# Attention rows in token order, and the first GLU tile's LayerNorm inside the last forward segment

## Chip, cores and metric

One core of a Trainium2 chip runs the whole program: forward and backward of one transformer block in one launch. The metric is the device time in us of that launch. The kernel before takes 3122.28 us (median of 3 runs, 3121.11 to 3123.98).

## The reference

The block has a recurrent attention with memory, and a gated GLU; both branches are modulated by a condition vector. The kernel gives the output and the gradients of all inputs. Cut to what matters here:

```python
# attention: 64 segments of 32 tokens; 8 memory rows go from each segment to the next
for s in range(n_seg):
    h = concat([mem, x[:, s*32:(s+1)*32]])            # 40 rows
    q, k, v = h@Wq, h@Wk, h@Wv                        # 32 heads of 128
    o = softmax(mask(q k^T * scale)) v @ Wo
    mem = o[:, :8]
    outs.append(o[:, 8:])                             # 32 rows of the branch's output
# block
h = layernorm(x) * (1 + ca) + sa
x = x + ga * attention(h)
h = layernorm(x) * (1 + cb) + sb
x = x + gb * ((sigmoid(h @ w_gate) * (h @ w_up)) @ w_down)
# and jax.vjp of all of it with grad_out
```

x is 1 x 2048 x 512, the GLU's inner width F is 1792, and all tensors are bfloat16.

## The kernel before, in words

The program has four stages: the forward loop over the segments (`phase2`), the GLU forward and backward (`phase3`), the backward loop over the segments (`phase4`) and the weight gradients of the attention (`phase5`).

**Forward loop.** 64 segments follow one another, since each needs the memory rows of the one before. A segment projects K, Q and V (L771 to L785), turns K and Q, multiplies and exponentiates (`st_exp`), sums and divides (`den`, `pv`, `ost`), turns the result (`ott`) and multiplies by Wo (`outproj`, L849). TensorE works on 32 rows a segment: the 8 memory rows and the first 24 tokens. The last 8 tokens of four segments are collected and multiplied together (`TailRows`). The result of a segment is split into a high and a low bfloat16 part (`split_pair`, at_hi and at_lo), folded (`sum_pair`), and in the next segment turned into rows and stored by `store_rows` (L336) through POOL's queue: 32 rows of a segment into `AOA`, and 32 tail rows of four segments into `AOB`. So the rows of one GLU tile of 128 tokens lie in eight pieces. The instructions of the forward loop keep the order of the program on each engine (`pin`, L894).

**Between the loops.** In segment 63 SP queues the four rows of the modulation, broadcast to 128 partitions in float32 (`mod_bc` of 2 to 5: ga, sb, cb, gb), and the loads of GLU tile 0 (L793 to L796). POOL queues the loads of w_down, w_up and w_gate into the memory of Wv and Wk, which the projections no longer need (L810 to L812). The last probabilities and values are turned on TensorE (L882 to L891), and the last tail rows are finished (L892).

**GLU.** 16 tiles of 128 tokens go through a software pipeline of seven steps s0 to s6; a round runs the deepest step first (`run_pipeline`). s0 loads the next tile (`glu_load`: dout, eight pieces of attention rows, x0), makes the residual x1 and its LayerNorm on DVE, and db = grad_out * gb on POOL. s1 turns h2 and db by DMA into hdT. s2 makes g and u (32 products of 448 columns for each tile, by L1039 and L1043), s3 the backward product du (L1062, evacuated by DVE in L1064), s4 the forward product by w_down and pr_gb = dout * b on DVE (L1089), s5 the product by the turned w_up and w_gate, and the LayerNorm's backward, s6 column sums in `acc_ps`. The backward products need w_down, w_up and w_gate turned: 168 turns of 128 x 128 on TensorE (`wdT_piece`, `wT_piece`), placed in s0 of tiles 0 to 2 (L974). In phase 3 only DVE, ACT and POOL are held behind the forward loop (`pin_behind`, L1182); the order of the rest comes from the scheduler of the build.

**After the GLU.** `accs` (L1183) takes the column sums out of PSUM and goes to DMOD. The memory of phase 3 is then used again, for the turned Wo (WoT) among others.

Of the kernel before, what the change touches and what calls it, by code (L numbers as in the profile page):

```python
# [10 lines left out]
ALU = mybir.AluOpType  # L11
# [29 lines left out]
class K:  # L41
# [43 lines left out]
    def alloc_dram(self):  # L85
# [6 lines left out]
        self.AOA = d("AOA", [NS + 1, 32, cfg.D], BF16)  # L92
        self.AOB = d("AOB", [NS // 4, 32, cfg.D], BF16)
# [231 lines left out]
    def store_rows(self, psp, pool, ft, dram, name, tag, then=None):  # L325
# [5 lines left out]
        def f():  # L331
            tp = psp.tile([128, 128], BF16, name=name + "_tp", tag=tag)
            nc.tensor.transpose(tp[:], tb[:], self.ident[:])
            rb = pool.tile([128, 128], BF16, name=name + "_rb")
            nc.vector.tensor_copy(rb[:], tp[:])
            nc.gpsimd.dma_start(dram.rearrange("r (c x) -> (r c) x", x=128), rb[:])  # L336
            if then is not None:
                then(rb)
# [93 lines left out]
    def phase2(self):  # L432
# [13 lines left out]
        with ExitStack() as ctx:  # L446
# [26 lines left out]
            nc.gpsimd.dma_start(self.AOA[0, 0:M, :], io["A_mem0"].rearrange("o m d -> (o m) d"))  # L473
# [174 lines left out]
            tail = TailRows(self, sb2, psp, psp, 1, "ao", self.AOB, 2, ptag="p")  # L648
# [20 lines left out]

            i0 = len(self.traced())  # L670
            for pi in range(NP):
                mask_mm(pi)
            for s in range(NS):
# [95 lines left out]
                if norms:  # L769
                    norms.pop()()  # L770
                proj("k", 0, "dve")  # L771
                proj("k", 1, "act")
                if s == 0:
                    for f in firsts["k"]:
                        f()
# [17 lines left out]
                if s == NS - 1:  # L793
                    for i in range(2, 6):
                        self.mod_bc(None, i, "", t=self.bcs[i])
                    self.glu_first = self.glu_load(0, nc.sync)  # L796
# [12 lines left out]
                else:  # L809
                    nc.gpsimd.dma_start(self.w_down, io["B_w_down"].rearrange("(fc p) d -> p fc d", p=128))  # L810
                    nc.gpsimd.dma_start(self.w_up, io["B_w_up"].rearrange("(c p) f -> p c f", p=128))
                    nc.gpsimd.dma_start(self.w_gate, io["B_w_gate"].rearrange("(c p) f -> p c f", p=128))  # L812
# [44 lines left out]
                parts = self.split_pair(sb2, at_ps, "at")  # L857
                tail.collect(s4, [OT])
# [11 lines left out]
                self.store_rows(psp, sb2, ft, self.AOA[s + 1], "at", "p")  # L870
# [9 lines left out]
                if s < NS - 1:  # L880
                    norms.append(norm)
            for pi in range(NP):  # L882
# [9 lines left out]
            tail.finish()  # L892
            nc.vector.tensor_scalar_add(self.bcs[4], self.bcs[4], 1.0)
# [18 lines left out]
    def glu_load(self, j, q):  # L912
        io, D = self.io, self.cfg.D
        r0, r1 = j * 128, (j + 1) * 128
        x0, a_rows, dout = self.ring_x0[j % 2], self.ring_a[j % 6], self.ring_dout[j % 7]
        q.dma_start(dout, io["grad_out"].rearrange("o s d -> (o s) d")[r0:r1, :])
        self.load_x_rows(a_rows, j, self.AOA[1:], self.AOB, q)
        q.dma_start(x0, io["A_x"].rearrange("o s d -> (o s) d")[r0:r1, :])
        return dict(x0=x0, a_rows=a_rows, dout=dout)

    def phase3(self):
# [9 lines left out]
        with ExitStack() as ctx:  # L931
# [32 lines left out]
            def wdT_piece(c):  # L964
                def f():
                    for f0 in range(0, FC, 7):
# [7 lines left out]
            pieces = {0: [wdT_piece(c) for c in range(DC)],  # L974
                      1: [wT_piece(w_up, w_upT, 0, 8, 0), wT_piece(w_up, w_upT, 8, 6, 0)],
                      2: [wT_piece(w_gate, w_gateT, 0, 8, 1), wT_piece(w_gate, w_gateT, 8, 6, 1)]}
# [3 lines left out]
            def load(j):  # L980
                if j >= NT or j in ins:
                    return
                ins[j] = self.glu_first if j == 0 else self.glu_load(j, nc.sync)

            def s0(j):
                r0, r1 = j * 128, (j + 1) * 128
                load(j + 1)
                for f in pieces.pop(j, []):
                    f()
                st = ins.pop(j)  # L990
                a_rows = st["a_rows"]
                t0 = sbp.tile([128, D], F32, name="t0", tag="f32tmp", bufs=5)
                nc.vector.tensor_tensor(t0[:], a_rows[:], ga_bc[:], op=ALU.mult)
                x1 = sbp.tile([128, D], F32, name="x1", bufs=4)
                nc.vector.tensor_tensor(x1[:], t0[:], st["x0"][:], op=ALU.add)
                sts = sbp.tile([128, 6], F32, name="st", bufs=2)
                nc.vector.bn_stats(sts[:], x1[:])
                mv = sbp.tile([128, 2], F32, name="mv", bufs=2)
                nc.vector.bn_aggr(mv[:], sts[:])
                ve = sbp.tile([128, 1], F32, name="ve3", bufs=2)  # L1000
                nc.vector.tensor_scalar_add(ve[:], mv[:, 1:2], EPS)
                rstd = sbp.tile([128, 1], F32, name="rstd2", bufs=6)
                i0 = len(self.traced())
                nc.gpsimd.tensor_tensor(rstd[:], ve[:], mhalf[:], op=ALU.pow)
                db = sbp.tile([128, D], BF16, name="db", bufs=2)
                nc.gpsimd.tensor_tensor(db[:], st["dout"][:], gb_bc[:], op=ALU.mult)
                self.pin(i0, [mybir.EngineType.Pool])
                nc.gpsimd.dma_start(self.DBROWS[r0:r1, :], db[:])
                xh2 = sbp.tile([128, D], BF16, name="xh2", bufs=5)
                xhf = sbp.tile([128, D], F32, name="xhf", tag="f32tmp", bufs=5)  # L1010
                nc.vector.tensor_scalar(xhf[:], x1[:], mv[:, 0:1], rstd[:, 0:1], op0=ALU.subtract, op1=ALU.mult)
                nc.scalar.activation(xh2[:], xhf[:], AF.Copy)
                h2a = sbp.tile([128, D], F32, name="h2a", tag="f32tmp", bufs=5)
# [1079 lines left out]
```

The softmax here doesn't subtract the row's maximum and nothing guards it: scores larger than these inputs give would overflow.

## Time and profile before

| | |
|---|---|
| time, median of 3 | 3122.28 us |
| span of the profiled execution | 3125.4 us |
| PE busy | 3004.2 us, 96% |
| DVE, ACT, POOL busy | 52%, 40%, 47% |
| DMA busy in the forward loop (60 to 980 us) | 0.80 to 0.81 of 16 engines |
| forward loop ends | about 995 us |
| last product of the GLU's pipeline | about 1380 us |

A line of a timeline gives the start and the duration in us, the engine, the line of the kernel, the operation, output and inputs, shapes and count, and in brackets how long the engine stood idle before it and what ended that. SPq is SP's queue of DMA issues. A line of the table by stage gives the stretch, its length, then busy us and number of instructions for PE, its weight loads (PEld), DVE, ACT and POOL, the granted clock of TensorE, the busy share of the DMA engines and GB/s. In names of tiles, Wv, Wk and Wq stand for everything that lies in their memory in the GLU: w_down, the modulation rows and the rings of x0 and attention rows in Wv, w_gate and w_up in Wk, the turned w_gate and w_up in Wq.

### The profile page before, as it was taken

How to read it: one execution, taken by the hardware profiler on the slowest of the kernel's cores; microseconds unless marked ns; L12 is line 12 of the kernel's file. 1: busy time of each engine (PE TensorE's matmuls, PEld its weight loads, DVE VectorE, ACT ScalarE, POOL GpSimd, SP SyncE). 2: the span in 40 equal slices, each digit the busy share in tenths (PEclk: the TensorE clock that was granted, in tenths of full speed). 3: DMA queues.
4: the chain of work that ended last, by engine and by line, in shares of the span. 5: the costliest groups of instructions: out<-in, count | busy, mean ns of one | idle time of the engine just before them, and what ended most of it. 6: DMA issues, size and time to landing. Idle time of an engine off the chain costs nothing.

```text
span 3125.4 us, 106126 instructions
## 1 busy us (share of the span) xinstructions
PE 3004.2 (96%) x43769; PEld 1838.1 (59%) x43845; DVE 1616.2 (52%) x3738; ACT 1264.6 (40%) x3053; POOL 1473.0 (47%) x2974
## 2 busy tenths in 40 slices
PE   5999999999998799989989999999999999999999
PEld 3666666666665444445567777777777754455454
DVE  4556656655654777733255555555655542322321
ACT  2555555555554433322155555555555530110111
POOL 3666666666665466531144444444444432233322
PEclk8999999999999899999999999999999999999999
DMA  8887788788787798898589999999999998666674
GB/s 295 214 214 199 205 214 212 204 207 213 205 207 237 177 214 219 202 267 271 185 218 244 240 248 242 244 243 248 244 239 244 243 270 285 201 202 213 196 234 147
DMA packets 844665, 703.54 MB, mean 225 GB/s; under 512 B 543794, under 2 KB 716370, under 8 KB 843796
## 3 DMA queue, kind: packets, MB, share of 16 engines
q1 hardware_dynamic: 714404, 486.69, 62.2%
q0 software_dynamic: 59120, 148.64, 14.6%
q10 hardware_dynamic: 70656, 61.41, 6.3%
q8 instruction: 345, 5.65, 0.8%
q14 instruction: 140, 1.15, 0.1%
HBM read 294.93 MB, written 276.35 MB: 183 GB/s over the span
## 4 chain that ended last, share of the span: by engine, by line
PE 50%; issue 4%; DMA 2%; POOL 1%; DVE 0%; SPq 0%; ACT 0%; POOLq 0%; DVEq 0%
PE gps L1885 10%; PE dh_ps L216 8%; PE g_ps L1547 6%; PE pass_ps L256 5%; PE gps5o L1899 4%; PE dhq_ps L224 4%; PE gps L1234 3%; PE dh_tps L216 3%; PE dp_ps L1526 2%; PE tps L1459 2%; PE dp_ps L1534 1%; PE turn_ps L1413 1%; PE dh_ft L321 1%; PE gps L1164 1%; PE wtp L1300 1%
## 5 line engine op out<-in xcount | busy, mean ns | idle before, releaser
L1885 PE MATMUL gps<-rows,hrows 128*128 128x512 bf16 (+2 forms) x2124 | 415.6, 355 | 1.9
L1885 PEld LDWEIGHTS <-hrows 128*128 128x128 bf16 x2160 | 211.2, 98 | 204.6
L256 PEld LDWEIGHTS <-hT 128*32 128x32 bf16 x6144 | 158.2, 97 | 161.3 <-issue 1.9
L1591 POOL COPY dOst<-RAd 96x512 bf16<-96x512 bf16 x128 | 75.4, 613 | 311.3 <-DVE RAd L63 311.1
L1889 POOL DMA_DIRECT2D out_dram<-ot x108 | 81.4, 754 | 258.6 <-DVE ot L63 132.3
L63 DVE CAST ot<-gps 128x512 bf16<-128x512 f32 (+3 forms) x76 | 48.1, 633 | 284.9 <-PE gps L1885 191.6
L875 POOL TENSOR_TENSOR Pst<-Pst,rden 120x1408 bf16<-120x1408 bf16 x63 | 159.6, 2533 | 57.4 <-issue 38.9
L61 ACT ACTIVATE ot<-gps 128x512 bf16<-128x512 f32 (+3 forms) x75 | 41.3, 551 | 356.2 <-PE gps L1885 225.3
L61 ACT ACTIVATE dVT<-g_ps 128x512 bf16<-128x512 f32 (+1 forms) x192 | 109.3, 569 | 95.9 <-PE g_ps L1547 95.5
L63 DVE CAST RA0v<-pass_ps 128x512 bf16<-128x512 f32 x128 | 88.5, 692 | 89.5 <-PE pass_ps L256 86.2
L216 PE MATMUL dh_ps<-WvT,dVT 128*32 128x512 bf16 x2048 | 133.4, 380 | 0.0
L256 PE MATMUL pass_ps<-Wv,hT 128*32 128x512 bf16 x2048 | 133.3, 380 | 0.0
L1899 PE MATMUL gps5o<-WoT,rows 128*128 128x512 bf16 x580 | 127.8, 379 | 1.0 <-DMA rows<-OSR 0.3
L224 PE MATMUL at_ps<-Wo,OT 128*32 128x256 bf16 x4096 | 125.0, 275 | 0.1
L256 PE MATMUL pass_ps<-Wk,hT 128*32 128x512 bf16 x2048 | 123.3, 383 | 1.5 <-ACT hT L865 1.1
L1536 DVE SCALAR_TENSOR_TENSOR dS<-dp_ps,Pst_l 128x512 bf16<-128x512 f32 (+1 forms) x192 | 112.0, 639 | 22.8 <-PE dp_ps L1534 22.8
L256 PE MATMUL pass_ps<-WoT,dyT 128*32 128x256 bf16 (+1 forms) x3072 | 122.4, 308 | 0.9 <-ACT dyT L1665 0.9
L224 PE MATMUL dhq_ps<-WqT,dQT 128*32 128x256 bf16 x4096 | 122.9, 273 | 0.0
L216 PE MATMUL dh_ps<-WkT,dKT 128*32 128x512 bf16 x2048 | 122.3, 380 | 0.0
L256 PE MATMUL pass_ps<-Wq,hT 128*32 128x512 bf16 x2048 | 121.6, 379 | 0.0
L224 PEld LDWEIGHTS <-dQT 128*32 128x32 bf16 x4096 | 109.6, 97 | 15.9
L709 ACT ACTIVATE ET<-st_ps 128x480 bf16<-128x480 f32 (+1 forms) x192 | 96.1, 535 | 42.6 <-ACT qT L61 34.7
(419 smaller groups left out, 7164.5 us busy)
## 6 DMA issues: line engine op xcount, KB each, us to landing
OSR<-Ost SPq DMA_DIRECT2D x64, 352.0 KB
OT<-OT SPq DMA_DIRECT2D x64, 352.0 KB
VT<-VTr SPq DMA_DIRECT2D x64, 352.0 KB
PS<-Pst SPq DMA_DIRECT2D x64, 352.0 KB
OT_l<-OT SPq DMA_DIRECT2D x64, 352.0 KB
Pst_l<-PS SPq DMA_DIRECT2D x64, 352.0 KB
VT_l<-VT SPq DMA_DIRECT2D x64, 352.0 KB
DVR<-rows_x POOLq DMA_DIRECT2D x64, 352.0 KB, 6.4
```

The source lines that it names most:

```text
L61: return nc.scalar.activation(out, in_, AF.Copy)
L63: return nc.vector.tensor_copy(out, in_)
L216: self.nc.tensor.matmul(ps[32 * j:32 * j + 32, :], lhsT=lhsT, rhs=w, start=(n < 4), stop=(n >= total - 4), tile_position=(0, 32 * j))
L224: nc.tensor.matmul(ps[32 * j:32 * j + 32, :], lhsT=x[k], rhs=w[k][:, 256 * d:256 * d + 256], start=(n == 0), stop=(n == total - 1), tile_p ...
L256: self.nc.tensor.matmul(ps[32 * j:32 * j + 32, :], lhsT=lhs(c), rhs=rhs, start=(c == 0), stop=(c == DC - 1), tile_position=(0, 32 * j))
L709: nc.scalar.activation(part3(ET, pi)[:, 0:n, 0:120], st_ps[:, 0:n, 0:120], AF.Exp, scale=cfg.scale)
L875: nc.gpsimd.tensor_tensor(Pst[0:120, :, :], Pst[0:120, :, :], rden[:, :].unsqueeze(2).to_broadcast([120, G, 128]), op=ALU.mult)
L1234: nc.tensor.matmul(ps[:], lhsT=h2r[:, j, c * 128:(c + 1) * 128], rhs=xr[:, j, :], start=(j == 0), stop=(j == NT - 1))
L1536: nc.vector.scalar_tensor_tensor(out=part3(dS, pi), in0=ps[:, 0:n, :], scalar=cfg.scale, in1=part3(Pst, pi), op0=ALU.mult, op1=ALU.mult)
L1547: nc.tensor.matmul(ps[:, j, :], lhsT=lh[:, g * GW:(g + 1) * GW], rhs=rh[:, g * GW:(g + 1) * GW], start=True, stop=True)
L1885: nc.tensor.matmul(ps[:, 0:ng * E], lhsT=hrows[:, tp_, c * 128:(c + 1) * 128], rhs=rows[:, tp_, 0:ng * E], start=(tp_ == 0), stop=(tp_ == ...
L1899: nc.tensor.matmul(pss[gg][:], lhsT=src[0][:, src[1], gg * E:(gg + 1) * E], rhs=dyrows[:, tp_, :], start=(tp_ == order[0]), stop=(tp_ == o ...
```

## The change

1. **Rows in token order.** `AOA` and `AOB` become `AOM` (the memory rows of each segment) and `AX` (all tokens in order). The stores go through SP: two for a segment, four for the tail of four segments. A GLU tile's attention rows are then one load instead of eight. The loads of `glu_load` are in the order x0, attention rows, dout.
2. **First tile inside segment 63.** LayerNorm and turns of GLU tile 0 (`glu_first`) are written into segment 63, behind the split of its attention result. They use memory of Wq, which is free after the Q projection. It is meant to have hdT of tile 0 ready before PE asks for it.
3. **Weights and turns reordered.** w_gate and w_up are loaded right after segment 63's K projection, w_down after its first P·V product. The turns come as w_gate, w_down, w_up, one part after each round of the pipeline, instead of w_down, w_up, w_gate in the first three rounds.
4. **Smaller moves.** `tail.finish` stands before the last turns; pr_gb moves from s4 to s5 (2 buffers instead of 3); `accs` lies in Wk's memory.

```diff
-        self.AOA = d("AOA", [NS + 1, 32, cfg.D], BF16)
-        self.AOB = d("AOB", [NS // 4, 32, cfg.D], BF16)
+        self.AOM = d("AOM", [NS + 1, cfg.M, cfg.D], BF16)
+        self.AX = d("AX", [cfg.S, cfg.D], BF16)
...
+            def rows_a(rb, s):
+                c_x = lambda t: t.rearrange("r (c x) -> (r c) x", x=128)
+                nc.sync.dma_start(c_x(self.AOM[s + 1]), rb[0:M * DC, :])
+                nc.sync.dma_start(c_x(self.AX[s * T:s * T + 32 - M, :]), rb[M * DC:128, :])
+            def rows_b(rb, b):
+                for i in range(4):
+                    t = (4 * b + i + 1) * T
+                    nc.sync.dma_start(self.AX[t - M:t, :].rearrange("r (c x) -> (r c) x", x=128), rb[32 * i:32 * i + 32, :])
...
-                if norms:
+                if s < NS - 1 and norms:
                     norms.pop()()
                 proj("k", 0, "dve")
                 proj("k", 1, "act")
+                if s == NS - 1:
+                    nc.gpsimd.dma_start(self.w_gate, io["B_w_gate"].rearrange("(c p) f -> p c f", p=128))
+                    nc.gpsimd.dma_start(self.w_up, io["B_w_up"].rearrange("(c p) f -> p c f", p=128))
+                    norms.pop()()
...
                 if s == NS - 1:
-                    for i in range(2, 6):
+                    self.glu_st = self.glu_load(0, nc.sync)
+                    for i in (2, 4, 3, 5):
                         self.mod_bc(None, i, "", t=self.bcs[i])
-                    self.glu_first = self.glu_load(0, nc.sync)
...
                     nc.gpsimd.dma_start(self.w_down, io["B_w_down"].rearrange("(fc p) d -> p fc d", p=128))
-                    nc.gpsimd.dma_start(self.w_up, io["B_w_up"].rearrange("(c p) f -> p c f", p=128))
-                    nc.gpsimd.dma_start(self.w_gate, io["B_w_gate"].rearrange("(c p) f -> p c f", p=128))
...
                 parts = self.split_pair(sb2, at_ps, "at")
+                if s == NS - 1:
+                    nc.vector.tensor_scalar_add(self.bcs[4], self.bcs[4], 1.0)
+                    self.glu_first(small)
                 tail.collect(s4, [OT])
...
-                self.store_rows(psp, sb2, ft, self.AOA[s + 1], "at", "p")
+                self.store_rows(psp, sb2, ft, lambda rb, s=s: rows_a(rb, s), "at", "p")
...
+            tail.finish()
             for pi in range(NP):
                 ps, n = transposes_part(ET, pi)
...
-            tail.finish()
-            nc.vector.tensor_scalar_add(self.bcs[4], self.bcs[4], 1.0)
...
+        q.dma_start(x0, io["A_x"].rearrange("o s d -> (o s) d")[r0:r1, :])
+        q.dma_start(a_rows, self.AX[r0:r1, :])
         q.dma_start(dout, io["grad_out"].rearrange("o s d -> (o s) d")[r0:r1, :])
-        self.load_x_rows(a_rows, j, self.AOA[1:], self.AOB, q)
-        q.dma_start(x0, io["A_x"].rearrange("o s d -> (o s) d")[r0:r1, :])
...
-            pieces = {0: [wdT_piece(c) for c in range(DC)],
-                      1: [wT_piece(w_up, w_upT, 0, 8, 0), wT_piece(w_up, w_upT, 8, 6, 0)],
-                      2: [wT_piece(w_gate, w_gateT, 0, 8, 1), wT_piece(w_gate, w_gateT, 8, 6, 1)]}
+            turns = {0: [wT_piece(w_gate, w_gateT, 0, 8, 1)], 1: [wT_piece(w_gate, w_gateT, 8, 6, 1)],
+                     2: [wdT_piece(c) for c in range(DC)],
+                     3: [wT_piece(w_up, w_upT, 0, 8, 0)], 4: [wT_piece(w_up, w_upT, 8, 6, 0)]}
...
-                pr = sbp.tile([128, D], BF16, name="pr_gb", bufs=3)
-                nc.vector.tensor_tensor(pr[:], st["dout"][:], b_bf[:], op=ALU.mult)
-                st.update(duT=duT, dgT=dgT, pr=pr)
+                st.update(duT=duT, dgT=dgT, b_bf=b_bf)
...
+                pr = sbp.tile([128, D], BF16, name="pr_gb", bufs=2)
+                nc.vector.tensor_tensor(pr[:], dout[:], st["b_bf"][:], op=ALU.mult)
...
             def after(it):
+                for f in turns.pop(it, []):
+                    f()
+                if it == 1:
+                    self.pin(i0, [mybir.EngineType.SP])
...
-            accs = sbp.tile([128, D], F32, name="accs", bufs=1)
+            accs = self.flat(self.Wk, 2 * DC * F, 2 * D, F32)
```

## The prediction, made before the change was run

> **What bounds the kernel now.** First the page: TensorE (PE) is busy for 96% of the span and its digit falls below 9 only at the start and around the end of the forward loop (990 us) and of the GLU (1390 us). So a change counts where PE is idle, and nowhere else. The table by stage sizes the first hole:
>
> ```profile
> core 0: us, PE busy (x) PEld busy (x) DVE busy (x) ACT busy (x) POOL busy (x), PEclk, DMA share, GB/s
> 500.00:980.00 480.00, 473.45 (x8899) 298.15 (x8899) 282.82 (x722) 254.65 (x684) 318.62 (x682) 1.00 0.81 208
> ...
> 990.00:1000.00 10.00, 7.39 (x154) 5.26 (x152) 5.17 (x12) 4.02 (x10) 4.03 (x6) 1.00 0.88 270
> 1000.00:1010.00 10.00, 5.65 (x57) 3.54 (x57) 2.11 (x5) 1.58 (x3) 0.00 (x0) 0.66 1.03 398
> 1010.00:1020.00 10.00, 6.65 (x81) 5.40 (x78) 7.17 (x17) 4.16 (x5) 1.85 (x4) 0.83 0.73 249
> 1020.00:1030.00 10.00, 3.56 (x50) 2.82 (x47) 8.46 (x15) 4.61 (x5) 5.03 (x7) 0.98 0.44 134
> 1030.00:1040.00 10.00, 3.57 (x11) 1.49 (x12) 6.49 (x11) 1.81 (x3) 3.51 (x6) 0.51 0.57 148
> ```
>
> In the forward loop PE is 98.6% busy, so nothing can be won there. From 990 to 1040 it is busy for 26.8 of 50 us: 23.2 us of hole, part of the rest at half clock. PE's timeline says what ends the idle times, in this hole and later:
>
> ```profile
> 1004.30 1.46 PE L969 MATMUL tp<-ident,Wv 128*128 128x128 bf16 x12 [6.43 <-DMA Wv<-in_B_w_down_dram]
> 1036.43 1.68 PE L1039 MATMUL mm<-Wk,hdT 128*128 128x448 bf16 x4 [10.08 <-DMA hdT<-h]
> 1067.47 1.65 PE L1043 MATMUL mm<-Wk,hdT 128*128 128x448 bf16 x4 [3.39 <-DVE du L1064]
> 1108.58 0.92 PE L1043 MATMUL mm<-Wk,hdT 128*128 128x448 bf16 x4 [1.17 <-DVE du L1064]
> 1389.19 1.01 PE L1313 MATMUL wtp<-ident,stage 128*128 128x128 bf16 x8 [4.34 <-DVE WoT L63]
> ```
>
> 6.4 us for the w_down load, 10.1 us for the turned rows of the first GLU tile, then a small wait in every GLU tile, and 4.3 us after the GLU (WoT on DVE waited 4.4 us for DMOD<-accs, says the table of waits). SP's timeline shows why the 10 us: h of tile 0 ends at 1024.65, but SP is busy with 8-issue row loads of later tiles and reaches its turn at 1034.
>
> ```profile
> 1030.66 0.30 SPq L358 DMA_DIRECT2D Wv<-AOB  x1
> 1031.07 1.21 SPq L1024 DMA_TRANSPOSE hdT<-db  x1
> 1032.33 0.54 SPq L357 DMA_DIRECT2D Wv<-AOA  x1
> ...
> 1033.98 1.19 SPq L1023 DMA_TRANSPOSE hdT<-h  x1
> ```
>
> DVE's timeline shows the per-tile wait: da and pr_gb stand ahead of du, and one of them is stretched.
>
> ```profile
> 1105.58 2.08 DVE L1127 TENSOR_TENSOR da<-dx,Wv 128x512 bf16<-128x512 f32 x1
> 1107.58 0.41 DVE L1089 TENSOR_TENSOR pr_gb<-Wk,b_bf 128x512 bf16<-128x512 bf16 x1
> 1107.91 2.20 DVE L1064 TENSOR_TENSOR du<-mm,sg 128x448 bf16<-128x448 f32 x4
> ```
>
> **What the Trainium skill says.** "SBUF — State Buffer", section "Who interferes with whom": a DVE instruction with two SBUF inputs and a GpSimd instruction that reads SBUF take one shared port pair, and the later of the two is fully blocked. The trace agrees: da takes 2.08 instead of 0.69 us, or pr_gb 1.38 instead of 0.41, always beside POOL's pr_ga (1.2 to 1.4 us). "DMA: Bandwidth & Descriptors", section "Issuing engines are not separate DMA queues": moving a DMA between SP and POOL changes only the issue time, since all run on the same 16 engines. The trace agrees in that both queues together stop near 400 GB/s (998 to 1010). "TensorE: Matmul & The Clock Gate", section "What's actually happening": PE idle for a few us runs at half clock for a while. Here: clock 0.66 and 0.51 in the two holes, and 1.68 us for products that take 0.92.
>
> **The change part by part.**
>
> Rows of attention in token order. POOL loses 79 store issues of 0.56 us; SP gains 192 stores (2 a segment, 4 more every fourth) and loses 7 of 8 row loads in 16 tiles. In the forward loop SP has a 5 us pause each segment (967.8 to 972.3, waiting for POOL's Pst), so 0.7 us more (2.1 in each fourth segment) lie in it. A store waits for at_rb on DVE, and behind it on SP stand OSR, OT and VT, which nobody needs for 10 us. Cost 0, bound 0 to 6 us if every segment slipped by 0.1. The bytes and rows of the DMA are equal.
>
> First LayerNorm inside segment 63. By the instruction order of the changed build PE does 16 turns of w_gate in segment 63, before its first P·V product (990.35), and waits there for w_gate. POOL issues w_gate at about 984.2 (after the K projection; now 992.3). Its 1792 KB take 4.6 us at 398 GB/s, or 12.7 us as w_down did (991.6 to 1004.3): landing 989.6 to 997.7. From 986 to 988 the DMA share is 0.04, so I take 992.5: PE stalls 2.2 us (0 to 7.3), and behind it stands the rest of segment 63. With 16 turns at 0.0765 us (8 in 0.61) the end of at_lo goes from 995.9 to 999.2.
>
> Behind at_lo DVE now has tile 0: 0.42 (1+cb), t0 0.68, x1 0.69, statistics 1.0, POOL's pow 0.76, xhf 1.38, h2a 0.67, h2 0.68: 6.3 us. It first waits for the MODROW broadcasts. In the kernel before these were issued at 991.5 to 995.2. By the semaphores in the build each load on SP waits for the load eight places earlier; the four loads eight behind the broadcasts are issued at 999.30, 1003.20, 1005.76 and 1008.99, so the broadcasts land about 3 us apart beside the weight loads. In the changed build they stand behind some 1.5 MB of row loads, issued from 989 (end of the V projection) on: I take landings of 1001, 1004, 1006.5, 1009 (bounds 3 us earlier, 4 later). So h2 at 1004 + 6.3 = 1010.3. POOL, in order, does db (needs gb, 1009, 1.15), two row stores (1.15) and only then the copy of the tail (0.41): 1011.8. PE's last tail product waits for that copy: 2.8, then split, fold and turn 3.0 (1010.0 to 1013.0 now): 1017.6. Pst on DVE 3.5 and the leading evacuations 1.5: the first GLU product at 1022.6 instead of 1036.4. The turned hdT, h2 + 2.5 = 1012.8, is no longer waited for.
>
> But turns are owed. Before, 48 of 168 were left after the first GLU tile's forward products (1044.16). In the changed build these products take 7.4 us warm and 40 turns between them 3.1: they end at 1033.1 with 105 turns left, 57 x 0.0765 = 4.4 us more. Gain 1044.2 - 1033.1 - 4.4 = 6.7 us. With w_gate and MODROW at their early ends it is 15, at their late ends 0.
>
> pr_gb goes behind du, dg and x in DVE's order of every tile. PE waits for du in 13 tiles: six at 1.17 (da stretched) and seven at 0.74 (pr_gb stretched), 12.2 us. Without pr_gb in front, the first kind still waits for da and wins 0.33; in the second du starts 1.3 us earlier and the wait is gone. All of the first kind: 4 us; all of the second: 12. Which op loses the port is decided by less than 0.4 us, so I take half of 12.2: 6 us. The 3.4 us wait at 1067 is a pr_gb of 5.31 us behind POOL's umh and o_sb; it leaves this place, but another two-input op of DVE can meet umh there: 2 us (0 to 3.4). Later pr_gb delays h2 and hh by 0.4 us, hidden since PE needs their turns over 2 us later.
>
> accs in Wk. WoT no longer lies on accs, so DVE need not wait 4.4 us for DMOD. But the H2ROWS load, on ACT's queue ahead of ACT's WoT copies, now lies on accs and waits for the same DMOD (landing 1388.1). PE goes on for some 2 us, then waits for ACT: 2 us (0 to 4.3).
>
> Sum: 6.7 + 6 + 2 + 2 = 16.7, so 3122.3 - 16.7 = 3105.6; I say 3105.
>
> **The rivals.** (1) More: early landings (15), all du waits gone (12), 3.4 and 4.3 fully: 34.7, which is 3087.6; not all ends will come together, so I put this case at 3092. For it: the idle DMA at 986 to 988. Against: the MODROW landings. (2) The hole only moves: w_gate stalls 7 us inside segment 63 and MODROW lands at 1012, so the transition wins nothing, and da stays the stretched op: 3122.3 - 4 - 1 = 3117. For it: weights and broadcasts share the 400 GB/s as before. (3) Slower: SP's added stores cost 0.1 us a segment (6.4), and the two holes grow by 4 us since DVE, POOL and PE stand in order behind late broadcasts, with nothing won at du: 3122.3 + 6.4 + 4 - 2 = 3131. Against: SP's 5 us pause; PE's idle share of 1.4% in the forward loop comes from at_hi, at_lo and hT, which SP doesn't touch.
>
> **How the numbers follow.** The forecast (3098 to 3111) 0.57, rival 1 0.15, rival 2 0.17, rival 3 0.11. 0.2% is 6.2 us: faster is below 3116.0, slower above 3128.5. Faster: 0.57 + 0.15 and a third of rival 2: 0.78; same 0.12; slower 0.10. The range 3089 to 3120 leaves out rival 3 and a tail of rival 1.
>
> **What would show it.** In the trace after: a wait of L1038 for w_gate near 990 (about 2 us), a DVE wait for MODROW ahead of tile 0 (about 5 us), the first GLU product near 1022 and not after hdT, GLU tiles of about 19.3 us instead of 20.1 and 19.7, and less than 2.5 us ahead of WoT. The prediction is wrong if the forward loop's period (14.08 us) changes, if the broadcasts land after 1008, or if da or another two-input op takes pr_gb's place at POOL's port.

## The result, and the profile after

The changed kernel takes 3141.72 us (median of 4 runs, 3138.13 to 3144.12); the kernel before, beside it on the same chip, 3123.13 us (3121.11 to 3127.37). The ratio is 1.0057, 95% interval 1.0039 to 1.0074: about 18 us slower. The forecast was 3105, with 3089 to 3120 as its range, so it was wrong in direction and size.

The profiled execution of the changed kernel has a span of 3136.1 us against 3125.4, 10.7 us of those 18. That execution is the quickest of its four, and the profiled one of the kernel before (3127.18 us) lies at the slow end of its runs, so what follows explains 10.7 us, and what the other 8 are made of no trace here shows. Four milestones (on PE's timeline the first mask product of the loop, the K projection of segment 63 and the first GLU product, on DVE's the copy of accs) cut the span into stages, and the table below says where the time went, in us:

| stage | before | after |
|---|---|---|
| first mask product of the loop to the K projection of segment 63 | 924.1 | 934.3 |
| from there to the first GLU product | 54.0 | 47.9 |
| from there to the copy of accs | 343.2 | 350.1 |
| from there to the end | 1745.8 | 1745.7 |

Nearly all of it, 10.2 us, is lost in the forward loop, in which I had costed the change at nothing. The start of the GLU gained 6.1 us and the GLU lost 6.9.

First the table by stage of the changed kernel, with the same columns as in the prediction:

```profile
core 0: us, PE busy (x) PEld busy (x) DVE busy (x) ACT busy (x) POOL busy (x), PEclk, DMA share, GB/s
500.00:980.00 480.00, 471.39 (x8822) 295.62 (x8824) 280.19 (x710) 250.05 (x671) 295.86 (x636) 1.00 0.86 206
1010.00:1020.00 10.00, 3.43 (x84) 1.96 (x76) 0.42 (x1) 0.38 (x1) 0.00 (x0) 0.76 0.98 318
1020.00:1030.00 10.00, 0.65 (x8) 0.30 (x12) 6.46 (x11) 1.11 (x2) 3.29 (x5) 0.50 0.65 208
```

In the loop PE does less in the same 480 us (8822 products for 8899) and the DMA engines are busier (0.86 for 0.81) while they move less (206 GB/s for 208). The second point is the important one, and the view of the DMA queues from 100 to 900 us has it more exactly: packets, MB, share of the 16 engines' time on SP's queue. Before:

```profile
q1 hardware_dynamic: 226500, 157.30, 76.8%
```

After:

```profile
q1 hardware_dynamic: 233519, 157.00, 81.8%
```

0.488% of the engines' time per MB before, 0.521% after: the same data has become 7% dearer. What waits for what in the loop is in the table of waits (us in total, times, longest). Before:

```profile
POOL Pst L875 <- issue: 38.9, 20, 3.1
...
POOL Pst L875 <- DMA Pst<-ET: 13.3, 14, 1.7
```

After:

```profile
POOL Pst L896 <- issue: 145.6, 43, 7.1
...
POOL Pst L896 <- DMA Pst<-ET: 51.5, 13, 6.5
...
PE or_ps L758 <- POOL Vst L803: 5.7, 9, 1.2
```

Before, PE never waited for POOL's Vst. So Pst's turn arrives late, POOL's Vst copy stands behind Pst in POOL's order, and PE's P·V product waits for Vst: 5.7 of the 10.2 us. (Of the rest, the wait for DVE's RA0v is 0.9 us, and PE's busy time in the loop is 2.9 us longer.) Why the turn is late shows on SP's timeline, here from one turn of VTr to the next:

```profile
794.32 1.47 SPq L822 DMA_TRANSPOSE VTr<-Vst  x1
...
798.20 3.27 SPq L661 DMA_DIRECT2D AX<-ao_b_rb  x4
801.56 0.36 SPq L654 DMA_DIRECT2D AOM<-at_rb  x1
...
812.47 1.58 SPq L822 DMA_TRANSPOSE VTr<-Vst  x1
814.16 2.56 SPq L828 DMA_TRANSPOSE Pst<-ET  x1
```

Between the two turns of VTr lie 18.15 us, and SP is issuing in all of them but for pauses of 0.1 to 0.4 us. Summed on SP's timeline between turns of VTr, over 15 groups of four segments, SP issues (us, in the four kinds of segment; the expectations below, written from another count, have 16.4 and 14.8 for the fullest kinds after):

| kernel | two kinds with k and q blocks | two kinds without | mean distance of the turns |
|---|---|---|---|
| before | 10.8, 11.4 | 8.9, 7.2 | 14.8 |
| after | 15.9, 14.3 | 10.6, 9.4 | 15.0 |

In the fullest kind of segment SP's work no longer fits into a segment: there the next turn comes 17.3 us later on average, where it came 14.7 us later before.

Then the transition and the GLU. PE's timeline of the changed kernel, with what ended each idle time:

```profile
1004.69 1.76 PE L1038 MATMUL tp<-ident,Wk 128*128 128x128 bf16 x16 [4.19 <-DMA Wk<-in_B_w_gate_dram]
...
1029.35 3.29 PE L216 MATMUL ao_tps<-Wo,ao_tail 128*32 128x512 bf16 x32 [15.92 <-POOL ao_tail L2014]
...
1040.36 1.33 PE L1089 MATMUL mm<-Wk,Wq 128*128 128x448 bf16 x3
...
1160.10 0.92 PE L1093 MATMUL mm<-Wk,hdT 128*128 128x448 bf16 x4 [0.84 <-DVE du L1114]
...
1397.35 0.71 PE L1367 MATMUL wtp<-ident,stage 128*128 128x128 bf16 x8 [1.66 <-DVE WoT L63]
```

The two waits of the old transition (6.4 us for w_down, 10.1 us for hdT) are replaced by 4.2 us for w_gate and 15.9 us for POOL's copy of the tail. SP's timeline shows where that one comes from: the broadcasts that feed the first LayerNorm stand behind the row loads of later tiles.

```profile
1000.12 6.51 SPq L937 DMA_DIRECT2D Wv<-AX  x3
1009.27 0.32 SPq L899 DMA_DIRECT2D PS<-Pst  x1
...
1016.73 1.75 SPq L367 DMA_DIRECT2D Wv<-MODROW  x4
```

In the GLU da is now the product that is held in each of the 13 tiles in which PE waits for du (DVE's timeline; POOL's pr_ga runs from 1258.47 to 1259.64 beside it):

```profile
1258.12 2.08 DVE L1177 TENSOR_TENSOR da<-dx,Wv 128x512 bf16<-128x512 f32 x1
1260.12 2.21 DVE L1114 TENSOR_TENSOR du<-mm,sg 128x448 bf16<-128x448 f32 x4
```

### The profile page after: what moved, and what is told of

Its sections match the earlier page's. It is cut to its first block, busy times and chain, and to the rows that moved or that the text cites. A ratio compares the mean times of both kernels' runs of the same rounds, so it can differ in the third digit from the quotient of the medians.

```text
span 3136.1 us, 105938 instructions
## 1 busy us (share of the span) xinstructions
PE 3002.5 (96%) x43769; PEld 1838.1 (59%) x43845; DVE 1616.2 (52%) x3738; ACT 1262.7 (40%) x3053; POOL 1434.1 (46%) x2895
## 3 DMA queue, kind: packets, MB, share of 16 engines
q0 software_dynamic: 56560, 146.01, 14.8%
## 4 chain that ended last, share of the span: by engine, by line
PE 48%; issue 4%; DMA 3%; POOL 1%; DVE 1%; ACT 0%; SPq 0%; POOLq 0%; ACTq 0%; DVEq 0%
PE gps L1939 9%; PE dh_ps L216 7%; PE g_ps L1601 6%; PE pass_ps L256 4%; PE gps5o L1953 4%; PE dhq_ps L224 4%; PE gps L1288 3%; PE dh_tps L216 2%; PE dp_ps L1580 2%; PE tps L1513 2%; PE dp_ps L1588 1%; PE turn_ps L1467 1%; PE dh_ft L321 1%; POOL out_dram L1943 1%; PE wtp L1354 1%
## 5 line engine op out<-in xcount | busy, mean ns | idle before, releaser
L63 DVE CAST ot<-gps 128x512 bf16<-128x512 f32 (+3 forms) x76 | 48.1, 633 | 258.5 <-PE gps L1939 169.1
L224 PEld LDWEIGHTS <-dQT 128*32 128x32 bf16 x4096 | 109.5, 97 | 15.9
```

The source lines that it names most:

```text
L63: return nc.vector.tensor_copy(out, in_)
L224: nc.tensor.matmul(ps[32 * j:32 * j + 32, :], lhsT=x[k], rhs=w[k][:, 256 * d:256 * d + 256], start=(n == 0), stop=(n == total - 1), tile_p ...
```

## The experiments

Stages of all of them, from their profiled executions, in us (columns as in the first table above; the last is the ratio to the kernel before, with its 95% interval). The time of the loop comes back to within a us or two: pr_only, accs_only and before_da don't touch it and took 923.3 to 924.0 in it, both_first and da_late leave it as in the changed kernel and took 932.5 and 933.8. The execution shown of small_192 is the slowest of its four.

| kernel | loop | to first GLU product | to accs | to the end | ratio |
|---|---|---|---|---|---|
| before | 924.1 | 54.0 | 343.2 | 1745.8 | 1 |
| after | 934.3 | 47.9 | 350.1 | 1745.7 | 1.0057 (1.0039–1.0074) |
| rows_pool | 924.2 | 49.5 | 350.3 | 1743.4 | 1.0004 (0.9996–1.0012) |
| rows_only | 925.3 | 47.6 | 351.1 | 1746.1 | 1.0003 (0.9995–1.0012) |
| sp_tight | 1009.2 | 55.3 | 341.5 | 1748.2 | 1.0269 (1.0253–1.0285) |
| sp_loose | 956.3 | 57.3 | 344.1 | 1749.1 | 1.0104 (1.0086–1.0121) |
| small_in_wq | 925.0 | 45.1 | 354.8 | 1744.4 | 1.0009 (1.0003–1.0016) |
| pad64 | 923.6 | 54.3 | 343.2 | 1745.8 | 1.0009 (1.0000–1.0017) |
| small_128 | 934.8 | 46.3 | 354.3 | 1744.7 | 1.0033 (1.0020–1.0046) |
| small_192 | 938.8 | 48.3 | 354.8 | 1748.8 | 1.0047 (1.0029–1.0065) |
| tail_one | 924.3 | 49.8 | 354.0 | 1746.4 | 1.0013 (1.0004–1.0022) |
| both_first | 933.8 | 39.9 | 355.1 | 1745.8 | 1.0030 (1.0017–1.0043) |
| da_late | 932.5 | 48.1 | 339.9 | 1746.9 | 0.9998 (0.9989–1.0007) |
| pr_only | 923.4 | 53.9 | 336.1 | 1745.9 | 0.9976 (0.9969–0.9984) |
| accs_only | 924.0 | 53.6 | 341.0 | 1748.5 | 0.9997 (0.9988–1.0006) |
| before_da | 923.3 | 53.1 | 326.7 | 1748.0 | 0.9946 (0.9929–0.9964) |
| best | 923.8 | 39.2 | 337.1 | 1742.0 | 0.9916 (0.9900–0.9933) |

### Is it SP's queue?

The first theory (A) was that SP's added stores fill its queue; its rival (B) that their packets slow everything, wherever they are issued.

**rows_pool**, the changed kernel with

```diff
-                nc.sync.dma_start(c_x(self.AOM[s + 1]), rb[0:M * DC, :])
+                nc.gpsimd.dma_start(c_x(self.AOM[s + 1]), rb[0:M * DC, :])
```

and the same for the two AX stores:

> The changed kernel with its 192 row stores issued on POOL instead of SP; all else as changed. Theory A (the SP queue is full in two of every four segments: it issues for 16.4 and 14.8 us there, of a segment of 14.8 to 15.0, and its late turn of Pst makes POOL's Pst, Vst and so PE late): SP falls back to about 11 us a segment, the K projection of segment 63 starts near 983 instead of 992.5, the wait of the P.V products for POOL's Vst copy is gone, and the time falls by about 10, to 3131 us (3128 to 3135). Theory B (the stores themselves, their packets of 256 B and their traffic, slow the other transfers, wherever they are issued): no change, 3138 to 3145. Theory C (POOL has no room either: 113 more issues at 0.5 us): slower than the changed kernel.

Measured: 3126.94 us, a little better than A expected, and the loop is back at 924.2. The same bytes, issued by POOL, cost nothing, so B falls and C (no room on POOL) too.

**rows_only**, the kernel before with the row part alone (stores on SP through rows_a and rows_b, one row load per GLU tile):

> The kernel before with the attention rows alone changed: stores in token order on SP, one row load per GLU tile. Theory A: the forward loop loses the same 10 us as in the changed kernel (K projection of segment 63 at 992). In the GLU the turn of the first tile's rows is no longer behind 8-issue row loads: of the 10.1 us wait some 6 come back. Together 3126 us (3122 to 3133). Theory B: also +10 in the forward loop. If the loss belonged to the first LayerNorm in segment 63 or to the pinned GLU order, the forward loop would stay at 982.5 and the time would be 3116.

Measured: 3126.54 us, as A said, but not for A's reason. The loop took 925.3 us: the same stores on SP lose about 1 us, not 10. This was the surprise of the study. In segments 0 to 62 all five engines have the same instructions in the same order, with the same semaphores, in this kernel and in the changed one, so the order of work can't be the difference. The GLU gave its part back, which is taken up below.

**sp_tight** and **sp_loose**, the kernel before with ten stores added in half of the segments; sp_loose has (3, 0) where sp_tight has (1, 2):

```diff
+                if s4 in (1, 2):
+                    for i in range(10):
+                        nc.sync.dma_start(self.DUM[i], self.ident[0:96, :])
                 nc.sync.dma_start(self.OSR[s], gl3(Ost))
```

> The kernel before with 10 added SP stores of a constant tile (96 x 128 bf16) to a scratch row in every segment of number 1 or 2 of its group of four, the two in which SP also stores the large k and q blocks; nothing reads them. Theory A: 10 x 0.45 us of issue bring SP from 10.9 and 11.4 us to 15.4 and 15.9 us, above the segment's 14.75, so time grows by 10 to 30 us (3132 to 3152), and PE waits for POOL's Vst. Theory B: the same growth in this kernel and in the next.

> The same 10 stores, in the segments of number 3 or 0 of the group instead: same count, bytes and packets. Theory A: SP comes from 8.9 and 7.0 us to 13.4 and 11.5 us, below 14.75, and nothing waits: 3122 to 3126 us. Theory B (traffic): as in the kernel before it, 3132 or more.

Measured: 3209.4 and 3158.56 us. The tight place costs 2.5 times the loose one (84 and 33 us, where 10 to 30 and nothing were expected), and the longest wait of PE in the loop of sp_tight is the one that came up in the changed kernel:

```profile
PE or_ps L743 <- POOL Vst L784: 34.7, 22, 2.3
```

The loose place was to be free and isn't. A store took 0.53 us there on average, not 0.45, and with what it adds to its neighbours SP's two loose kinds went from 8.9 and 7.2 to 15.9 and 14.7 us. But the longest wait of PE in the loop of sp_loose is another one, for a tile of DVE that waits for a DMA:

```profile
DVE Ost L755 <- DMA OSR<-Ost: 17.5, 16, 2.2
...
PE tps L726 <- DVE Ost L755: 15.5, 16, 2.0
```

OSR, the store of Ost, stands on SP right behind the ten added stores, and the next segment can't write Ost before that store has landed. sp_tight has this wait too (PE's is 12.0 us there), and the changed kernel doesn't. So the pair shows that added issues cost by what stands behind them, and more in the fuller segments. How full SP can be, it doesn't tell.

### What differs between rows_only and the changed kernel

What differs in the loop is addresses. The changed kernel has a constant tile of 64 bytes per partition for the first LayerNorm, `glu_small`, ahead of the weights and of the loop's buffers, and moves them all up by 64 bytes. As built, ET, both Vst, Ost and VTr begin on multiples of 256 bytes in the kernel before and in rows_only, and 64 bytes behind such in the changed kernel. (Not every buffer of the loop did: Pst, which its turn writes, begins 160 bytes behind one before, and at_rb, which the row stores read, 32.) Theory D: the move makes transfers dearer, and only move and stores together overfill SP.

**small_in_wq**, the changed kernel with that tile elsewhere:

```diff
-            small = self.const.tile([128, 16], F32, name="glu_small")
+            small = self.flat(self.Wq, 2 * cfg.DC * cfg.F, 32, F32)
```

> The changed kernel with its 64-byte-per-partition scratch tile for the first LayerNorm put into the Q weights' free columns, so that every buffer behind the constants lies 64 bytes lower, at the addresses that it had in the kernel before. In the forward loop all five engines have the same instructions in the same order. Theory D (the rows on SP cost little by themselves, as the kernel with the rows alone showed; the 64 bytes that push all later buffers make each transfer of SBUF dearer, 0.52 instead of 0.49 per cent of the DMA engines' time per MB, and only both together overfill SP): the K projection of segment 63 comes about 925 us after the first mask product instead of 934, and the time is about 3132 (3129 to 3135). Theory A' (the last segment's changed work reaches back into the loop, the address is nothing): no change, 3138 to 3145.

Measured: 3128.3 us, loop 925.0. Against the changed kernel nothing in the loop differs but the addresses in SBUF, and 9.3 of its 10.2 us are back. Its DMA queue:

```profile
q1 hardware_dynamic: 237227, 159.02, 78.3%
```

0.492% per MB. **pad64**, the kernel before with an unused tile of the same size:

```diff
+            pad = self.const.tile([128, 16], F32, name="pad")
+            nc.gpsimd.memset(pad[:], 0.0)
```

> The kernel before with a constant tile of 64 bytes per partition added ahead of the loop's buffers and used by nothing. Theory D: the transfers' share per MB rises from 0.49 to about 0.52 per cent, SP's issues get longer but stay under the segment's time, since the rows are still stored by POOL: the forward loop grows by 0 to 3 us, 3122 to 3128. If the address alone cost what the changed kernel lost: 3132. If the address is nothing: 0.49 per cent and 3122 to 3126.

Measured: 3127.19 us, loop 923.6, and in its DMA view

```profile
q1 hardware_dynamic: 226645, 157.44, 81.8%
```

0.520% per MB: the move makes the transfers dearer by itself. What it costs in time by itself is 2.8 us by the ratio, with an interval of 0 to 5, and nothing in the loop of the trace. The four kernels make a table of two by two, with the mean issue of the turn of Pst, what SP issues in its two full kinds of segment, and the loop:

| | rows on POOL | rows on SP |
|---|---|---|
| old addresses | before: 1.84 us; 10.8, 11.4; 924.1 | small_in_wq: 1.82; 14.4, 13.3; 925.0 |
| 64 bytes further | pad64: 2.14; 12.3, 12.4; 923.6 | after: 2.19; 15.9, 14.3; 934.3 |

SP's load grows by each part about alike wherever it is added: by 3.6 and 1.9 us through the rows, by 1.5 and 1.0 us through the 64 bytes. Time doesn't, until the two together take the fullest kind past the segment's 14.8 us. Theory A' (the last segment's work reaching back into the loop) falls.

**small_128** and **small_192**, the changed kernel with that tile 128 and 192 bytes wide (32 and 48 columns):

```diff
-            small = self.const.tile([128, 16], F32, name="glu_small")
+            small = self.const.tile([128, 32], F32, name="glu_small")
```

> The changed kernel with its scratch tile 128 instead of 64 bytes wide, so that the later buffers lie 128 bytes behind their addresses in the kernel before. If it is the place within 128 bytes that makes the transfers dear: the DMA share per MB is 0.49 to 0.50 per cent, the issue of the turn of Pst takes about 1.8 us, the K projection of segment 63 comes 925 us after the first mask product, 3128 to 3132. If any move off the old addresses (a place within 256 or 512 bytes) does it: 0.52 per cent, 2.2 us, 934 us, 3138 to 3145.

> The same with 192 bytes, which is 64 bytes off within 128 again. If the place within 128 bytes counts: as in the changed kernel, 0.52 per cent per MB, turn of Pst 2.2 us, 934 us, 3138 to 3145. If 64 bytes were special for another reason (the neighbour of one buffer): 925 us and 3128 to 3132.

Measured: 3139.42 and 3142.52 us, loops 934.8 and 938.8, 0.518 and 0.519% per MB, turn of Pst 2.15 and 2.12 us. So the place within 128 bytes is not it; 64, 128 and 192 bytes are about equally bad. The Trainium skill has a rule that may be the reason: "DMA: Bandwidth & Descriptors", section "How a descriptor splits into AXI transactions", says that a transaction must start on a multiple of 256 bytes, so that a descriptor that doesn't start on one is read from the boundary below, with bytes that nobody uses. The packets of the changed kernel's loop are mostly under 512 bytes (187291 of 244932 from 100 to 900 us). An estimate from that section would be 10, 12 and 14 beats instead of 8 for 256 bytes at 64, 128 and 192 bytes off; the runs show one step of 6 to 7% and no such grading. The traces do show which packets became dearer: those of 256 bytes, 70% of SP's queue from 100 to 900 us, took 28.3 ns on average before and 32.3 in pad64, while those of 2816 bytes stayed at 119.6 and 118.8. But the median of the 256-byte packets is 18 ns in both; what grew is the share of those over 22 ns, from 6 to 14%, so it isn't the same addition for each packet either. That the three moves are bad and the old places good is shown, the section's reason is not. A move of 256 bytes, which would be harmless by that section, doesn't fit into SBUF and wasn't tried.

**tail_one**, the changed kernel, 64 bytes and all, with the four tail stores as one:

```diff
-                for i in range(4):
-                    t = (4 * b + i + 1) * T
-                    nc.sync.dma_start(self.AX[t - M:t, :].rearrange("r (c x) -> (r c) x", x=128), rb[32 * i:32 * i + 32, :])
+                to = self.AX[4 * b * T:4 * (b + 1) * T, :].rearrange("(i t) (c x) -> i t c x", i=4, x=128)
+                nc.sync.dma_start(to[:, T - M:T, :, :].rearrange("i t c x -> i (t c) x"), rb[:])
```

> The changed kernel, 64 bytes and all, with the four tail stores of every fourth segment made one store of the same bytes and packets. If the count of issues on SP is what costs beside the dearer transfers: SP's issue time falls by 3 x 0.78 us per four segments, 12.7 to 12.1 us a segment, in the very segment that was fullest (16.4 to 14.1 us), most of the forward loop's loss goes (926 to 929 us), 3130 to 3136. If the bytes and packets cost, not the issues: no change, 3138 to 3145.

Measured: 3130.15 us, loop 924.3, SP's two full kinds at 14.5 and 13.9 us; transfers as dear as in the changed kernel (0.518% per MB). Three issues less in every fourth segment take away the whole loss of the loop. It is the time that SP spends on issues in the fullest segment, not the bytes.

### The transition

**both_first**, the changed kernel with two orders altered: the tail copy ahead of the first LayerNorm, and the GLU's work on SP behind the MODROW loads (mod_last is the last of them):

```diff
+                tail.collect(s4, [OT])
                 if s == NS - 1:
                     nc.vector.tensor_scalar_add(self.bcs[4], self.bcs[4], 1.0)
                     self.glu_first(small)
-                tail.collect(s4, [OT])
...
+            self.pin_behind(i0, self.mod_last, [ET.SP])
```

> The changed kernel with two orders altered at the end of the forward loop: the copy of the last tail rows on POOL ahead of the first LayerNorm, and the MODROW broadcasts on SP ahead of the row loads for GLU tiles 1 to 5. Theory T (PE's 15.9 us idle time at 1013 to 1029 is POOL's copy and DVE's fold standing in order behind the LayerNorm, and that behind the late broadcasts, issued at 1016.7): broadcasts land near 1010, the first GLU product comes 8 to 14 us earlier after the K projection of segment 63 (34 to 40 us instead of 47.9), and the time falls by 4 to 12 us, to 3134 (3129 to 3138). Rival U (the weights and rows fill the DMA up to 1015 either way, and the turns owed inside the GLU take the gain back): first product at most 4 us earlier, 3138 to 3143.

Measured: 3134.26 us. The first GLU product comes 8.0 us earlier, as theory T said, but the GLU takes 5.0 us longer, and the broadcasts didn't land near 1010: both theories were partly right. PE no longer waits for POOL's copy, yet it waits for the next in line, ACT's ao_b_hi, released late because DVE stands in order behind the same broadcast:

```profile
1022.48 0.28 PE L321 MATMUL ao_b_ft<-foldsel,ao_b_hi 128*128 128x32 bf16 x4 [10.05 <-ACT ao_b_hi L310]
```

```profile
1016.25 0.43 DVE L879 TENSOR_SCALAR Wv<-Wv 128x512 f32<-128x512 f32 x1 [6.84 <-DMA Wv<-MODROW]
```

(The first is PE's timeline, the second DVE's.) The broadcasts were issued at 999.17 to 1001.3 and the one awaited landed at 1016.2: issued 17.5 us earlier than in the changed kernel, landed 5.3 us earlier. The DMA share is 1.02 to 1.03 from 1000 to 1015 us of this run; the broadcasts share it with three weight loads of 1792 KB. That they would have to be issued before the weights is a conclusion from this, and not tried.

### The GLU tiles

**da_late**, the changed kernel with da behind du:

```diff
+                def da_f():
+                    nc.vector.tensor_tensor(da[:], dx1[:], ga_bc[:], op=ALU.mult)
+                    nc.gpsimd.dma_start(self.DAROWS[r0:r1, :], da[:])
...
                     nc.vector.tensor_tensor(du[:, sl], dp[:, 0:CH], sg[:, sl], op=ALU.mult)
+                while owed:
+                    owed.pop()()
```

> The changed kernel with da, the product that stands ahead of du on DVE and is held to 2.08 us beside POOL's pr_ga, moved behind du in each GLU tile. If PE's 0.84 us wait in every tile is da's: 12 waits of 0.84 and one of 2.46 go, the tile falls from 19.81 to about 18.97 us, and the time by 9 to 12 us, to 3131 (3129 to 3134). If another product takes its place at the port, or PE then waits for h or for da's turn instead: 3138 to 3143.

Measured: 3125.35 us, better than expected: 18 us below the changed kernel by the two ratios, 10.6 by the traces, which the intervals allow. PE's waits for du, 12.7 us in the changed kernel, are down to this in the table of waits, and the GLU is 10.2 us shorter:

```profile
PE mm L1094 <- DVE du L1115: 0.5, 1, 0.5
```

**pr_only**, the kernel before with pr_gb behind du and nothing else:

> The kernel before with pr_gb alone moved behind du, dg and x. The prediction's step: 4 to 12 us less and the wait at tile 1 gone. Rival V (from the changed kernel's tiles: da is now always the product held at POOL's port, PE waits 0.84 us in every tile where it waited 1.17 in six and 0.74 in seven, so 12.2 us become 10.9, and a wait of 2.5 us takes the place of the 3.4): 0 to 3 us less than before, 3123 to 3126.

Measured: 3118.94 us, 7.5 us less by the ratio. The rival is refuted and the prediction's step confirmed, alone, but for the wait at tile 1, which went from 3.4 to 2.1 us and not away. PE's waits for du fell from 16.3 us to

```profile
PE mm L1043 <- DVE du L1064: 8.3, 9, 2.1
```

with six early tiles at 0.83 (da held) and of the later ones only one in the table, at 0.52, since there pr_gb had been the one held. In rows_only, where pr_gb is where it was, the same view reads

```profile
PE mm L1058 <- DVE du L1079: 20.8, 14, 3.6
```

with da held in all these tiles (1.18 us in most). So the row part puts every tile into the kind in which moving pr_gb wins little. How it does that stays open: in both kinds POOL's pr_ga starts 0.35 us after da (1165.97 and 1166.32, 1245.64 and 1245.99 before), and only the winner of the port differs. The prediction's reading that the trace agrees with "the later of the two is fully blocked" holds only in part: in the six early tiles the one held is da, which by these starts is the earlier.

**accs_only**, the kernel before with

```diff
-            accs = sbp.tile([128, D], F32, name="accs", bufs=1)
+            accs = self.flat(self.Wk, 2 * DC * F, 2 * D, F32)
```

> The kernel before with accs alone moved into the Wk columns. The prediction's step: PE's wait of 4.3 us for WoT on DVE shrinks, 2 us less (0 to 4.3). Rival W (the same PE time comes back as waits for the Wo and Wv weight loads behind it, as in the changed kernel, where accs to the end took 1745.7 us against 1745.8): PE's wait for WoT shrinks and accs to the end stays at 1745 to 1746, 3125 to 3127.

Measured: 3124.85 us, no change. PE's wait for WoT on DVE fell from 4.3 us to 1.1, but a wait of 1.2 us for ACT's WoT came in, and PE's wait for the Wv load behind it grew from 0.6 to 2.5. The copy of accs, the milestone, came 2.2 us earlier and what follows it took 2.7 us longer, so the two stages together are unchanged (2089.0 and 2089.5). Rival W is right about the time, though not about the stage to the end.

### What beats both

**before_da**, the kernel before with pr_gb and da behind du, has no part of the change but pr_gb's place; **best** is the changed kernel with small_in_wq, rows_pool, both_first and da_late together.

> The kernel before with both pr_gb and da behind du in each GLU tile, nothing else. If da and pr_gb at POOL's port are all of PE's wait for du: the 13 waits (12.2 us) and that of 3.4 us at tile 1 go, a tile falls to 18.97 us, and the time by 11 to 16 us, to 3113 (3110 to 3116).

> The changed kernel with the five edits of the earlier runs together: scratch tile in the Q weights' columns, row stores on POOL, da behind du, the tail copy on POOL and the broadcasts on SP ahead of the first LayerNorm and of the later row loads. From the stages of those runs: mask to the K projection of segment 63 924, to the end of the GLU 397.9 - 10 - 3 = 385, to the end 1745, with 57.5 ahead: 3112 (3107 to 3118). If the parts don't add (the turns owed inside the GLU take the early start back): 3116 to 3120, and then no better than the kernel before with da moved.

Measured: 3111.33 and 3100.78 us (14.7 and 25.3 us below the kernel before beside them). best was expected at 3112, and at 3107 at the least. From the K projection of segment 63 to accs it took 376.2 us instead of the 385 that the parts add up to: where both_first gave 5.0 of its 8.0 us back in the GLU, best gave nothing back (39.2 and 337.1 us against 48.1 and 339.9 in da_late); from there to the end it took 1742.0 instead of 1745. Why the early start is kept once da is out of the way was not tried apart.

## Why the prediction was wrong

**Rows in token order: "Cost 0".** This step failed, and it decided the sign. Three things in it were wrong. The "5 us pause each segment (967.8 to 972.3)" was read in the last group of four segments, the only one that stores no k and q blocks; two of four segments elsewhere issue 10.8 and 11.4 us, and their longest pauses, in the middle of the loop (600 to 700 us), are 2.8 to 2.9 and 2.0 to 2.4 us. The added issues were put at 0.7 us a segment (2.1 in each fourth); by small_in_wq they bring 3.6 and 1.9 us to the two full kinds. And the 64 bytes of glu_small were not costed at all, because I looked for what the change adds to the queues and not for what it moves in SBUF; the section on transactions quoted above was a reason to look. Each alone left the loop within 1.2 us of the old time, so the bound of 6 us was fair for either alone, and wrong for the two together. The step's words that nobody needs what stands behind the stores "for 10 us" overlooked that the next turns of VTr and Pst stand behind it too; and as sp_loose shows, the next segment needs OSR. I also set the period at 14.08 us, which is the distance of two late K projections; the mean by the turns of VTr is 14.8.

The Trainium skill's sentence that another issuing engine saves only the issue time ("DMA: Bandwidth & Descriptors", section "Issuing engines are not separate DMA queues") holds here to the letter, the loop being the same with rows on POOL, and was misread: the issue time was the scarce thing.

**Rival 3** had the sign and 3131 us. Its 6.4 us through SP was the nearest to what happened (10.2); the place it named against itself, SP's pause, is the reading that failed. Its other half, holes that grow by 4 us, didn't come: the transition won 6.1 us. The three signs of being wrong that the prediction named all came: the mean distance of the turns went from 14.8 to 15.0 us, the broadcast that DVE waits for landed at 1021.6, and da took pr_gb's place.

**First LayerNorm inside segment 63.** The mechanism was right, the landing mis-sized. Counted from the K projection of segment 63: w_gate stalled PE 4.2 us (predicted 2.2, 0 to 7.3); the (1+cb) broadcast landed at +29.1 (predicted +21.5); POOL's tail copy came at +36.4 (+29.3), and the first GLU product at +47.9 (+40.1), so 6.1 us early instead of 13.8. The chain from broadcast over db and the row stores to the copy and to PE ran as written, 7 to 8 us late. What the owed turns cost was mis-sized as well: 4.4 us in the prediction, from PE's own time of a turn; in the changed kernel PE also waits 8.7 us for their evacuations on DVE and ACT (2.9, 2.6, 2.0 and 1.2 in the table of waits from the first GLU product on; before, there is no such wait). These 8.7 us, less the 3.6 us by which the waits for du fell, are the larger part of the 6.9 us that this stage lost. rows_pool, small_in_wq, tail_one and both_first too start the GLU 4 to 14 us earlier than the kernel before and take 7 to 12 us longer in it, with 5.2 to 7.2 us of such waits; what the rest is stays open. Of this step's forecast gain of 6.7 us, and the 8 of the next, the two stages together show minus 0.8.

**pr_gb behind du: gain 6 (4 to 12), and 2 for the early wait.** Right alone: pr_only gained 7.5 us. In the changed kernel the 6 didn't come: all 13 tiles have da held, 12.7 us of waits where the same tiles had 12.2, since one of them waits 2.5 us. The early wait of 3.4 us did go, so all waits for du went from 16.3 to 12.7. The lower end of 4 us was also mis-worked: it takes 0.33 from each of 13 waits of 1.17, but 7 of the 13 had only 0.74 to begin with, so the first kind everywhere means 13 x 0.84 = 10.9, a gain of 1.3 at most. Against rows_only, where all tiles are of the first kind, the 0.33 is right (1.18 and 0.84).

**accs in Wk: 2 us (0 to 4.3).** The wait shrank and the time didn't: the lower end. ACT's wait, which the step named, was 1.2 us of it; the wait for the Wv load, which it didn't name, grew by 1.9.

## What to carry to other kernels

Before adding issues to a queue, sum its issue time in each kind of iteration, in the middle of the loop and not at its end, and compare the fullest kind with the period; what is nearly free until then can cost all at once after it (1 us and 10 us here). When a change adds or resizes a buffer, however small, see which buffers it moves, and where the ones that DMA reads and writes come to lie: here three moves off multiples of 256 bytes each made the transfers 6 to 7% dearer. A wait that moves from one engine to the next in order (hdT, then the tail copy, then the fold) is not removed until the transfer behind it is earlier.

## What the runs showed that I had not expected

A constant tile of 64 bytes that nothing reads raises the DMA engines' time per MB from 0.488 to 0.520% and the issue of a DMA turn from 1.84 to 2.14 us. Ten stores of 24 KB in every second segment cost 84 us or 33 us according to the segments they are put in. And two engines whose instructions keep the same 0.35 us distance share a port with one winner in some tiles and the other in the rest, for whole stretches of tiles; what decides it, these runs don't show.
